# Recurrent attention with a wave-mixing layer on one core: weight loads without gating copies, weight tables in halves, and a new written order

## The chip, the cores and the metric

The kernel runs on one core of a Trainium2 chip. The core has a matmul engine (PE, with its weight loads PEld), a vector engine (DVE), an activation engine (ACT), GpSimd (POOL) and a sync engine that here only issues transfers (SP). SP and POOL each have a queue of transfers of their own; the transfers of both run on the core's 16 DMA engines. The metric is device time in microseconds; of several runs the median counts.

## The reference

The first part is a linear attention with decay, over 4 batches, 8 heads, 768 steps and heads of 48:

```python
for t in range(S):
    kt, vt, rt = (k[:, :, t], v[:, :, t], r[:, :, t])
    cur = np.einsum('bhd,bhe->bhde', u[None] * kt, vt)
    y[:, :, t] = np.einsum('bhd,bhde->bhe', rt, state + cur)
    state = w[None, :, :, None] * state + np.einsum('bhd,bhe->bhde', kt, vt)
```

Its result, x of 768 tokens by 384 columns in each batch, goes through a mixing layer:

```python
theta = x @ w_theta
zr, zi = x * np.cos(theta), x * np.sin(theta)
y = np.einsum('ts,bsd->btd', w_tok_r, zr) + np.einsum('ts,bsd->btd', w_tok_i, zi)
u = x + y
return u + np.maximum(u @ w_ch, 0.0)
```

## The kernel before

**The attention** goes over the tokens in chunks of 128, two chunks (a pair) at a time, three pairs in a batch (`front`). For each pair SP loads k and v in two transfers each and r in one. Kw is k times a table of inverse powers of w (`wpinv`), Rw is r times a table of powers (`wpow`), both in bf16 (L457, on POOL or DVE as the order says). PE transposes them (L416), ACT or DVE copies the transposes out as KT and RT (L206, L207). The scores KT by RT (L487) are masked by DVE into mAT (L492). PD is RT times KT (L497), from which PE makes the diagonal term dg (L504), and yd is dg times vb (L512), vb being v in bf16. The state grows by Kw by vb (L525), a DVE step (L539 or L541), a product with w^128 (L547) and two copies Sb in bf16 (L206, L207). The output y is RT by Sb (L560) and mAT by vb (L569) added up in one PSUM bank, and DVE adds yd to give x (L583). x is transposed, multiplied by Wth (theta, L605), ACT takes sine and cosine (L609), and DVE makes the two products z (L612).

**The mixing** (`mixing`) multiplies z by the transposed token weights WrT and WiT (L641) into uT (L652), then by Wch (L685); DVE adds the result to the transposed uT (L690) and SP stores it. Batch 0 mixes in single tiles of 128 tokens, so a tile needs only its own tile of WrT and WiT; the others mix 384 or 256 tokens at once.

**The weights.** POOL loads Wth and Wch (L384) and twelve tiles of token weights into six staging buffers (L395), casting them to bf16 on the way. PE transposes each tile (L402), ACT or DVE copies it out to WrT or WiT. None of these loads has an input to wait for. In the version before, a one-column copy from a loaded buffer into the destination (`after`, L375 to L379) makes the first load of each buffer wait: Wth for the first half of v of pair 0, six staging buffers and Wch for the first half of k of pair 2 of batch 0.

**The tables.** w is spread over the partitions by one matmul (L274), ACT takes the logarithm (L314) and three exponentials, `wpinv` and two of `wpow` (L319).

**The order.** Each piece of work is a task with a number, given in the order of the code. `ORDER`, a string that a search on a model of the chip wrote, lists the tasks in the order in which they are emitted, with the engine of each (P, V for DVE, A, G for POOL, S) and the PSUM banks of those that need one. Each engine runs its own tasks in that order, each when its inputs are there. A list entry such as `187G` is a whole task: here the load of a weight tile. POOL tasks that share a port with DVE (`port=True`) also wait for the last such DVE task that stands before them in the string (L135 to L138). The load buffers form a ring of ten, so a load of a later batch waits until the buffer has been read.

In the old string POOL's first fourteen entries are identity, iota, pads, mask, the first products Kw and Rw and a small one; then the copies and Wth, and the token loads behind a yd. SP's list begins with k, k, r of pair 0, then k, k, r of pair 1, r and a k of pair 2, and then v of pair 0.

Of the kernel before, what the change touches and what calls it, by code (L numbers as in the profile page):

```python
# [33 lines left out]
111P32 114P 112P 70P6 147P5 107V 144V 115V 113V 183G 170G 171G 108G 175G 148V 139A 76A 75A 71A 109A 150P4
151V 152G 154A 153A 72A 140P02 116P7 145V 117V 216S 188P3 192P5 142V 141V 110G 118P4 122P1 149G 189A 119A
193A 120A 77V 73V 124A 155P72 156P 158P 180P6 367P0 184P3 368P 185A 123A 159V 157V 181V 172P5 160P2 215S
214S 217S 261S 218S 262S 263S 265S 310S 264S 309S 206G 209G 200G 173A 360P4 361P 176P7 121V 203G 220G 161V
125V 222V 221V 219V 15G 162P6 166P3 353P1 177A 362P 354P 363P 355P 225P2 163A 164A 168A 167A 165V 169V 223P5
369P 370P 364P 226A 227A 224V 234V 231P76 232V 228P32 365P 356P 357P 238P5 366V 233V 239V 242V 266G 268G
235P7 371P 372P 241A 229V 267G 240G 270P4 373V 230V 376P6 358P 359V 236A 207P5 246P7 249P 247P3 210P0 378P2  # L40
374P1 271A 208V 403P4 201P5 377V 211A 202A 404P 405P 406P 407P 408P 204P6 311S 312S 313S 426S 473S 213G 197G
194G 375A 269V 237V 250V 248V 379A 205A 409V 316G 396P0 272P5 414P1 251P7 397P 398P 399P 400P 401P 243V 274G
273A 252A 244A 281V 285P2 275P34 278P65 314G 402V 282P7 286V 287G 245A 283A 288A 276V 290V 415A 280V 277V
253P0 412P7 254A 255A 257P3 318P2 315G 289G 317G 279V 294P15 258A 259A 383P4 384V 260V 386P0 295P 198P6
320P3 319A 321A 291G 284G 293A 292A 322A 413A 199V 195P4 380P2 297P 196V 387V 381V 296V 298V 389P6 390P 391P
392P 393P 394P 256V 299P4 395V 329V 333P3 326P02 323P15 419P7 385S 388S 382S 334V 324V 300A 301P6 330P4 303A
420V 327V 325V 328V 422P3 410P1 416P7 305P0 425S 335G 432G 337G 336A 302A 331A 430G 429S 428S 306A 304V 307A
438A 411V 423V 417V 332G 474S 472S 421S 424S 427S 418S 475S 521S 476S 619S 620S 522S 520S 621S 523S 524S
338P64 339P 434P5 341P 574P2 564P0 565P 569P1 449P3 599P7 342V 340V 343P4 435A 479G 570P 344A 480V 478V 477V
450V 453V 308V 483P5 481P6 349P4 482V 484A 345P3 604P5 600P 351A 350A 347A 346A 433V 431V 486P64 575P 436P3  # L50
352V 348V 451A 437A 492V 576P 577P 571P 601P 493P3 572P 487V 454G 456A 485A 494A 566P 445V 578V 488V 573V
527G 623S 489P62 442P34 496P1 452A 495G 490V 567P 446P6 605P 497V 491V 498G 568V 443V 602P 444V 501V 603V
583P2 457P0 447A 455A 448G 528G 526G 584A 499A 606P 607P 500A 608V 439P63 441V 440V 579P2 505P41 460P 581P7
508P 506P 591P5 525G 624G 502G 504G 625G 626G 582V 531P3 458P6 529P7 592V 580A 532A 533A 509V 507V 461V 459V
585P2 588P5 530A 622S 594P1 595P 462P3 510P4 586V 589V 631A 511A 503A 463V 540V 534P06 537P27 544P5 642P3
545V 546G 627G 548A 547A 596P 597P 541P4 468P5 542A 538V 536V 598V 643V 535V 539V 543G 646V 549P26 469A 470A
629P4 630A 464P1 550P 593S 667S 671G 645G 516P0 552P 512P5 610P7 551V 553V 466A 465A 513A 514A 587S 590S
628S 665S 609S 666S 673V 467V 471V 554P3 632P42 635P16 675P5 555A 634V 515V 644G 670G 672G 518A 517A 560P3
556P2 676A 561A 558A 562A 557A 636V 637V 611V 633V 647V 563V 638V 668S 669S 713S 712S 755P0 756P 765P1 650P5
616P6 780P7 781P 760P3 653P 613P4 639P2 766P 761P 559V 519V 614V 677A 640V 617V 641V 688P4 767P 689V 768P  # L60
654V 769V 651P2 790P6 719G 690V 717G 762P 763P 782P 783P 693V 652V 764V 784V 648A 649A 694G 696G 692A 691G
695A 612S 674S 684V 615S 618S 714S 681P51 678P42 682V 683V 680V 679V 791P 792P 685P3 793P 697P75 757P 758P
794V 759V 718G 720G 722P1 698P 686A 687G 785P3 700P 786P 787P 723A 699V 701V 715S 716S 724G 721S 731V 735P2
736V 728P46 725P01 774P7 732P5 656S 661P2 788P 655S 729V 730V 727V 726V 789V 733A 737G 738G 739G 740P45 743P
657P6 741P 771P1 734G 744V 702S 704P0 799P3 802P5 662A 663A 659A 658A 703S 708P2 706A 705A 770S 664V 742V
660V 746S 707V 777P6 810P4 796P0 709A 710A 775V 772V 778V 711V 805P7 806P 811P 751P2 815P1 752A 753A 745S
795S 773S 779S 776S 754V 747P6 816P 845P2 846P 748A 749A 750V 830P6 812P 813P 807P 808P 817P 818P 797V 803V
800V 814V 809V 819V 831P 835P0 847P 848P 840P5 841P 842P 836P 849V 854P3 862P4 843P 832P 833P 837P 838P 855V
863V 834V 844V 839V 824P7 821P1 827P2 850P3 852P4 856P6 798S 804S 801S 820S 825V 822V 828V 864S 826S 823S
829S 859P5 865P0 851A 853A 857V 860V 866V 858S 861S 867S  # L70
# [73 lines left out]
def kernel(  # L144
# [120 lines left out]
    def setup():  # L265
# [3 lines left out]
        def wu_fill(e):  # L269
# [4 lines left out]
        P.add((PE, 1300), lambda e: nc.tensor.matmul(bank("w")[:, :HD], ones, w_row, start=True,  # L274
                                                     stop=True),
              rd=["w_row", "ones"], acq=["w"], prio=-100, mode=3)
# [31 lines left out]
        def mask(e):  # L308
# [5 lines left out]
        P.add((ACT, 450), lambda e: nc.scalar.activation(  # L314
            lw_f, bank("w")[:, :HD], Act.Ln), rd=["tab0"], use=["w"],
              wr=["lw_f"], prio=-97.9)
        for j, (dst, col, key) in enumerate(((wpinv, 1, "wpinv"), (wpow[:, 0], 2, ("wpow", 0)),
                                             (wpow[:, 1], 3, ("wpow", 1)))):
            P.add((ACT, 520), lambda e, dst=dst, col=col: nc.scalar.activation(  # L319
                dst, lw_f, Act.Exp, scale=tok_f[:, col:col + 1]),  # L320
                rd=["lw_f", "tok_f"], wr=[key], prio=-97.7 + 0.1 * j)
# [51 lines left out]
    nstage, gate = [0], []  # L373

    def after(dst, load_key, key, prio):  # L375

        _, i, c = load_key
        P.add((POOL, 90), lambda e: nc.gpsimd.tensor_copy(dst, Ls[i][:, c * HD:c * HD + 1]),
              rd=[load_key], wr=[key], prio=prio, port=True)  # L379

    def weights(src, dst, key, prio, load_key):
        s3 = src.rearrange("(o p) n -> p o n", p=C)
        after(dst[:, 0, 0:1], load_key, key, prio)
        P.add((POOL, 850), lambda e: nc.gpsimd.dma_start(out=dst, in_=s3), wr=[key], prio=prio,  # L384
              dma=1700, kind="sw", port=True)

    def token_weights(prios, load_key):
        for to in range(NCH):
            for src, dst, key in ((moe_w_tok_r, WrT, "WrT"), (moe_w_tok_i, WiT, "WiT")):
# [3 lines left out]
                if nstage[0] <= 6:  # L393
                    after(stg[i][:, 0:1], load_key, ("stg", i), prio - 10)
# [34 lines left out]
    def front(b, base):  # L429
# [3 lines left out]
        for pr in range(NP):  # L433
# [10 lines left out]
            if b == 0 and pr == 0:  # L444
                load_wu()
                small_tables()
                weights(moe_w_theta, Wth, "Wth", -50, ("L", iv, 0))
            if b == 0 and pr == 2:
                gate.append(("L", ik, 0))
            for c in range(2):  # L450
                for src, tab, tk_, dst, key in (
                        (Ls[ik].rearrange("p (c h d) -> p c h d", c=2, h=H)[:, c], wpinv, "wpinv",
                         Kw, kK),
                        (Ls[ir].rearrange("p (h c d) -> p c h d", c=2, h=H)[:, c], wpow[:, c],
                         ("wpow", c), Rw, kR)):
                    P.add([(POOL, pool_ns(HD)), (DVE, dve_ns(HD))],
                          lambda e, c=c, src=src, tab=tab, dst=dst: eng_of[e].tensor_mul(  # L457
                              dst[:, c, :, :D], src, tab.rearrange("p (h d) -> p h d", h=H)),
                          rd=(L2(ir) if dst is Rw else [("L", ik, c)]) + [tk_], wr=[key + (c,)],
                          prio=pb, port=True)  # L460
# [241 lines left out]
    token_weights([20 + 4 * i for i in range(NCH)], gate[0])  # L702
    weights(moe_w_ch, Wch, "Wch", 50, gate[0])
# [37 lines left out]
```

## Time and profile before

| | |
|---|---|
| time, median of 3 runs | 136.4 us (136.21 to 136.49) |
| the profiled execution's own time | 137.21 us |
| its span | 135.5 us |
| PE busy | 122.2 us, 90% |
| DVE busy | 114.2 us, 84% |
| ACT busy | 78.0 us, 58% |
| POOL busy | 68.8 us, 51% |
| DMA moved | 24.65 MB, mean 182 GB/s |
| SP's queue (q1), POOL's queue (q0) | 21.44 MB and 2.95 MB |
| a k or v transfer, an r transfer | 192 KB, 384 KB |
| a token weight tile, Wth or Wch | 192 KB, 288 KB |

A busy share is the time in which an engine had an instruction in work. PE's time includes matmuls that wait in its pipeline. A row of the timeline gives the start, the duration, engine, line, operation, output, input and count of a group of instructions, and in brackets how long the engine was idle before it and what released it. In a row of busy time by stage stand the stage, its length, the busy time and instructions of PE, PEld, DVE, ACT and POOL, the granted clock, the mean share of the DMA engines (above 1 where transfers overlap) and GB/s. In a row of a DMA queue stand packets, MB, and the time of its packets as a share of the 16 engines' time in the window.

### The profile page before, as it was taken

The page shows a single profiled execution, that of the slowest core. Times are in us where ns is not written, and L with a number is a line of the kernel's source. Part 1 is how long each engine was busy: PE and PEld are TensorE (multiplying, and loading weights), DVE is VectorE, ACT ScalarE, POOL GpSimd, SP SyncE. Part 2 cuts the span into 40 slices and gives each one's busy share as a digit, 9 for nine tenths or more (in the row PEclk, how much of TensorE's full clock was granted, in tenths as well). Part 3 has the DMA queues.
Part 4 walks back from the last instruction along what each step waited for, and adds up shares of the span by engine and source line. Part 5 has one row for each costly group of instructions (what it writes and reads, how often), then busy time and mean ns, then how long its engine had stood idle before and what let it go on. Part 6 is the DMA issues. An engine that isn't in the chain of part 4 may idle for free.

```text
span 135.5 us, 4188 instructions
## 1 busy us (share of the span) xinstructions
PE 122.2 (90%) x1667; PEld 91.9 (68%) x1667; DVE 114.2 (84%) x231; ACT 78.0 (58%) x145; POOL 68.8 (51%) x104
## 2 busy tenths in 40 slices
PE   3358778979999999999999999999999999999990
PEld 1136665858989987977766687776566676577950
DVE  5279989798999869998999999999999997575581
ACT  3665868798836779858387339799411337240020
POOL 7324477767658456548205999755249860000000
PEclk9999999999999999999999999999999999999999
DMA  4999999999998993399999977997989439734945
GB/s 78 225 252 203 192 186 258 222 217 190 238 211 198 192 188 63 137 204 237 244 193 229 254 139 200 151 202 148 223 220 203 97 69 112 171 119 174 92 171 177
DMA packets 79781, 24.65 MB, mean 182 GB/s; under 512 B 74257, under 2 KB 79762, under 8 KB 79762
## 3 DMA queue, kind: packets, MB, share of 16 engines
q1 hardware_dynamic: 76400, 21.44, 75.4%
q0 software_dynamic: 2528, 2.95, 13.1%
q8 instruction: 13, 0.21, 0.6%
q10 hardware_dynamic: 834, 0.00, 0.3%
q14 instruction: 6, 0.05, 0.1%
HBM read 20.06 MB, written 4.72 MB: 183 GB/s over the span
## 4 chain that ended last, share of the span: by engine, by line
PE 68%; DVE 14%; DMA 8%; issue 3%; ACT 2%; SPq 1%; POOL 1%; DVEq 0%; POOLq 0%
PE bank L641 31%; PE bank L416 11%; PE bank L685 7%; PE bank L605 5%; DMA stg<-in_moe_w_tok_r_dram 5%; PE bank L487 4%; DVE mAT L492 4%; DMA ld<-in_r_dram 4%; PE bank L525 3%; PE bank L569 2%; PE bank L402 2%; PE bank L560 2%; ACT RT L206 2%; DVE z L612 1%; DVE fin L690 1%
## 5 line engine op out<-in xcount | busy, mean ns | idle before, releaser
L641 PEld LDWEIGHTS <-z 128*128 128x128 bf16 x468 | 34.3, 98 | 11.1 <-DVE z L612 0.4
L641 PE MATMUL bank<-WrT,z 128*128 128x128 bf16 (+2 forms) x234 | 31.8, 264 | 0.2 <-DVE z L612 0.2
L641 PE MATMUL bank<-WiT,z 128*128 128x128 bf16 (+2 forms) x234 | 31.8, 264 | 0.0
L492 DVE TENSOR_TENSOR mAT<-bank,mask 128x512 bf16<-128x512 f32 x48 | 31.0, 679 | 0.2 <-PE bank L487 0.2
L457 POOL TENSOR_TENSOR Kw<-ld,wpinv 128x384 bf16<-128x384 f32 x17 | 17.1, 1012 | 14.5 <-DVE yd L512 5.4
L612 DVE TENSOR_TENSOR z<-sc,x 128x768 bf16<-128x768 bf16 x24 | 14.2, 604 | 2.5 <-ACT sc L609 2.5
L605 PE MATMUL bank<-Wth,xT 128*128 128x384 bf16 x72 | 15.5, 334 | 0.9 <-DVE xT L207 0.6
L609 ACT ACTIVATE sc<-bank,pi 128x384 bf16<-128x384 f32 x24 | 13.9, 588 | 4.2 <-PE bank L605 3.5
L206 ACT ACTIVATE Sb<-St 64x192 bf16<-64x192 f32 x29 | 10.3, 358 | 9.8 <-DVE St L547 3.7
L206 ACT ACTIVATE RT<-bank 128x1024 bf16<-128x1024 bf16 x12 | 12.3, 1027 | 6.1 <-PE bank L416 6.0
L652 DVE TENSOR_TENSOR uT<-bank,xT 128x384 bf16<-128x384 f32 (+1 forms) x25 | 13.0, 534 | 2.9 <-PE bank L641 2.7
L685 PE MATMUL bank<-Wch,uT 128*128 128x384 bf16 (+2 forms) x75 | 14.7, 319 | 0.0
L512 POOL TENSOR_TENSOR yd<-dg,vb 128x768 bf16<-128x768 f32 x9 | 13.3, 1475 | 0.7 <-ACT sc L609 0.6
L547 POOL TENSOR_TENSOR St<-Ta,wC 128x192 f32<-128x192 f32 x12 | 6.7, 556 | 13.4 <-DVE Ta L541 6.2
L583 DVE TENSOR_TENSOR x<-bank,yd 128x384 bf16<-128x384 f32 x24 | 12.3, 549 | 1.4 <-POOL yd L512 0.8
L457 POOL TENSOR_TENSOR Rw<-ld,wpow 128x384 bf16<-128x384 f32 x12 | 11.9, 1002 | 2.5 <-DVE Rw L457 2.3
L609 ACT ACTIVATE sc<-bank 128x384 bf16<-128x384 f32 x24 | 11.4, 494 | 1.8 <-PE bank L605 1.8
L690 DVE SCALAR_TENSOR_TENSOR fin<-bank,un 128x384 f32<-128x384 f32 x21 | 10.8, 548 | 0.9 <-DMA un<-uT 0.7
L487 PE MATMUL bank<-RT,KT 64*128 64x128 bf16 x192 | 9.2, 235 | 2.0 <-ACT RT L206 2.0
L206 ACT ACTIVATE un<-bank 128x384 bf16<-128x384 bf16 x8 | 3.7, 484 | 11.7 <-PE bank L416 11.7
L497 DVE TENSOR_TENSOR PD<-RT,KT 128x1024 bf16<-128x1024 bf16 x12 | 8.2, 686 | 2.0 <-ACT RT L206 1.9
L206 ACT ACTIVATE KT<-bank 128x1024 bf16<-128x1024 bf16 x7 | 7.1, 1021 | 4.2 <-PE bank L416 4.2
(81 smaller groups left out, 199.6 us busy)
## 6 DMA issues: line engine op xcount, KB each, us to landing
ld<-in_k_dram SPq DMA_DIRECT2D x24, 192.0 KB, 4.6
ld<-in_r_dram SPq DMA_DIRECT2D x12, 384.0 KB, 4.8
ld<-in_v_dram SPq DMA_DIRECT2D x24, 192.0 KB, 4.7
out_dram<-fin SPq DMA_DIRECT2D x21, 192.0 KB, 2.0
stg<-in_moe_w_tok_r_dram POOLq DMA_DIRECT2D x6, 192.0 KB, 5.6
stg<-in_moe_w_tok_i_dram POOLq DMA_DIRECT2D x6, 192.0 KB, 5.5
out_dram<-stg SPq DMA_DIRECT2D x2, 192.0 KB, 1.9
Wth<-in_moe_w_theta_dram POOLq DMA_DIRECT2D x1, 288.0 KB, 5.7
```

The costliest lines, as they stand in the source:

```text
L206: return nc.scalar.activation(o, i, Act.Copy)
L416: nc.tensor.matmul(bank16(tok)[:, i * C:(i + 1) * C], s, ident, is_transpose=True, start=(i == 0), stop=(i == n - 1))
L457: lambda e, c=c, src=src, tab=tab, dst=dst: eng_of[e].tensor_mul(dst[:, c, :, :D], src, tab.rearrange("p (h d) -> p h d", h=H)),
L487: nc.tensor.matmul(bank(tk[hi])[:, hp * C:(hp + 1) * C], KT[q, c, hp, :], RT[q, hp, c, :], start=(hp == 0), stop=(hp == HP - 1))
L492: P.add((DVE, dve_ns(HP * C)), lambda e, hi=hi, tk=tk, mAT=mAT: nc.vector.tensor_mul(mAT[:, hi], bank(tk[hi]).rearrange("p (h t) -> p h t" ...
L512: lambda e, yd=yd, dg=dg, vb=vb: eng_of[e].tensor_mul(yd.rearrange("p a h d -> p (a h) d"), wide(dg, D), vb.rearrange("p a h d -> p (a h) ...
L605: nc.tensor.matmul(bank(th)[:, :HD], xT[:, dk, to * C:(to + 1) * C], Wth[:, dk, :], start=(dk == 0), stop=(dk == ND - 1))
L609: P.add((ACT, act_ns(HD) - 5 + 95 * (1 - ri)), lambda e, th=th, sc=sc, ri=ri: nc.scalar.activation(sc[:, ri], bank(th)[:, :HD], Act.Sin, * ...
L612: P.add((DVE, dve_ns(2 * HD, 2.0)), lambda e, sc=sc, to=to: nc.vector.tensor_mul(z[:, to], sc, bc(x[:, to], 1, 2)), rd=[("x", xi, to), ("s ...
L641: nc.tensor.matmul(bank(tm)[:, q * n * C:(q + 1) * n * C], z[:, so, ri, dk * C:(dk + 1) * C], WT[:, so, w], start=(s0 == 0 and ri == 0 and ...
L652: nc.vector.tensor_add(uT[:, dks[0]:dks[-1] + 1, w0:w1], bank(tm)[:, :len(dks) * (w1 - w0)].rearrange("p (d t) -> p d t", d=len(dks)), xT[ ...
L685: nc.tensor.matmul(bank(tf)[:, :(d1 - d0) * C], uT[:, dk, j * C:(j + 1) * C], Wch[:, dk, d0 * C:d1 * C], start=(dk == 0), stop=(dk == ND - 1))
```

## The change

Three things change. The `after` copies go, eight in all, with the arguments that named the load to wait for. The matmul that spreads w, the logarithm and `wpinv` are cut into two halves of columns, each half with a task of its own (`wpow` stays whole); Kw then waits for both halves of `wpinv`. And the order string is replaced.

```diff
-        P.add((PE, 1300), lambda e: nc.tensor.matmul(bank("w")[:, :HD], ones, w_row, start=True,
-                                                     stop=True),
-              rd=["w_row", "ones"], acq=["w"], prio=-100, mode=3)
+        halves = [slice(i * (HD // 2), (i + 1) * (HD // 2)) for i in range(2)]
+        for i, q in enumerate(halves):
+            P.add((PE, 650), lambda e, i=i, q=q: nc.tensor.matmul(
+                bank("w%d" % i)[:, q], ones, w_row[:, q], start=True, stop=True),
+                rd=["w_row", "ones"], acq=["w%d" % i], prio=-100, mode=3)
...
+        for i, q in enumerate(halves):
+            P.add((ACT, 290), lambda e, i=i, q=q: nc.scalar.activation(
+                lw_f[:, q], bank("w%d" % i)[:, q], Act.Ln), rd=["tab0"], use=["w%d" % i],
+                wr=[("lw_f", i)], prio=-97.9)
+        for dst, col, key, q, rd in [(wpinv[:, q], 1, ("wpinv", i), q, [("lw_f", i)])
+                                     for i, q in enumerate(halves)] + [
+                (wpow[:, j], 2 + j, ("wpow", j), slice(0, HD), [("lw_f", 0), ("lw_f", 1)]) for j in range(2)]:
...
-    def after(dst, load_key, key, prio):
-
-        _, i, c = load_key
-        P.add((POOL, 90), lambda e: nc.gpsimd.tensor_copy(dst, Ls[i][:, c * HD:c * HD + 1]),
-              rd=[load_key], wr=[key], prio=prio, port=True)
...
-        after(dst[:, 0, 0:1], load_key, key, prio)
...
-                if nstage[0] <= 6:
-                    after(stg[i][:, 0:1], load_key, ("stg", i), prio - 10)
```

The new string, read as tasks, differs in these places. POOL's list begins with three pads, iota, identity and a pad; then come the loads of WrT tile 2 and WiT tile 0, two pads, the loads of WrT tile 0, Wth and WiT tile 2, the mask, and only then the first Rw. WrT and WiT tile 1 follow behind vb of pair 0, tile 3 behind state products of pair 1, tiles 4 and 5 behind yd of pair 2. SP's list begins with k, k, r of pair 0, then r, k, k of pair 1, v, v of pair 0, v, v of pair 1, and then pair 2. PE's list has the transposes of Rw of both first pairs ahead of the first scores, and the first weight transpose among the scores of pair 1; its first mixing stands ahead of the KT transposes of pair 2. DVE's list has the first products z behind one Rw of pair 2, where the old list had much of pair 2 ahead of them. Between engines, three vb casts move from ACT to POOL, three Kw from POOL to DVE and three Rw from DVE to POOL, and a few copies and a state product trade places.

More of the change, by code (lines that the diff above doesn't have):

```diff
@@ L34 @@
[L34 to L48, printed above, removed]
@@ L313, in setup @@
         P.add((POOL, 600), mask, wr=["mask"], prio=-95)
[L314 to L321, printed above, removed]
+        for i, q in enumerate(halves):
[5 more added lines that the diff above has]
+                (wpow[:, j], 2 + j, ("wpow", j), slice(0, HD), [("lw_f", 0), ("lw_f", 1)]) for j in range(2)]:
+            P.add((ACT, act_ns(q.stop - q.start, False) + 105), lambda e, dst=dst, col=col, q=q: nc.scalar.activation(
+                dst, lw_f[:, q], Act.Exp, scale=tok_f[:, col:col + 1]),
+                rd=rd + ["tok_f"], wr=[key], prio=-97.7)
     def small_tables():
@@ L446, in front @@
                 small_tables()
-                weights(moe_w_theta, Wth, "Wth", -50, ("L", iv, 0))
-            if b == 0 and pr == 2:
-                gate.append(("L", ik, 0))
+                weights(moe_w_theta, Wth, "Wth", -50)
             for c in range(2):
                 for src, tab, tk_, dst, key in (
-                        (Ls[ik].rearrange("p (c h d) -> p c h d", c=2, h=H)[:, c], wpinv, "wpinv",
+                        (Ls[ik].rearrange("p (c h d) -> p c h d", c=2, h=H)[:, c], wpinv, ("wpinv", 0),
                          Kw, kK),
@@ L458, in front @@
                               dst[:, c, :, :D], src, tab.rearrange("p (h d) -> p h d", h=H)),
-                          rd=(L2(ir) if dst is Rw else [("L", ik, c)]) + [tk_], wr=[key + (c,)],
+                          rd=(L2(ir) if dst is Rw else [("L", ik, c), ("wpinv", 1)]) + [tk_], wr=[key + (c,)],
                           prio=pb, port=True)
@@ L701 @@
     front(0, 0)
-    token_weights([20 + 4 * i for i in range(NCH)], gate[0])
-    weights(moe_w_ch, Wch, "Wch", 50, gate[0])
+    token_weights([20 + 4 * i for i in range(NCH)])
+    weights(moe_w_ch, Wch, "Wch", 50)
     for b in range(B):
```

75 lines of the change are left out of this document (45 added, 30 removed).

## The prediction

> **What bounds the kernel now.** I read the page's head and chain first, then busy time by stage, then the chain piece by piece.
>
> ```profile
> span 135.5 us, 4188 instructions
> PE 68%; DVE 14%; DMA 8%; issue 3%; ACT 2%; SPq 1%; POOL 1%; DVEq 0%; POOLq 0%
> ```
>
> ```profile
> core 0: us, PE busy (x) PEld busy (x) DVE busy (x) ACT busy (x) POOL busy (x), PEclk, DMA share, GB/s
> 0.00:10.00 10.00, 4.04 (x26) 2.30 (x26) 5.00 (x16) 5.45 (x7) 4.98 (x18) 1.00 0.84 182
> 10.00:20.00 10.00, 7.83 (x114) 6.55 (x109) 9.28 (x20) 6.92 (x11) 5.05 (x12) 1.00 1.02 195
> 20.00:33.00 13.00, 11.61 (x184) 9.01 (x182) 11.53 (x24) 11.19 (x22) 9.09 (x15) 1.00 1.18 223
> 33.00:82.00 49.00, 48.96 (x791) 39.59 (x789) 45.19 (x90) 32.27 (x61) 30.19 (x35) 1.00 0.90 192
> 82.00:98.00 16.00, 16.00 (x209) 10.95 (x207) 15.95 (x32) 13.43 (x26) 9.07 (x12) 1.00 1.03 192
> 98.00:132.00 34.00, 33.74 (x359) 23.51 (x358) 26.66 (x56) 8.76 (x19) 10.45 (x13) 1.00 0.74 142
> ```
>
> From 33 us on PE has no gap. From 82 to 98 DVE has none either (15.95 of 16.00), and there the chain runs over DVE. So the kernel is a ramp of 33 us and then a wall of PE work, with DVE just keeping up. The change alters neither the mixing nor any other matmul behind the ramp; it can gain in the ramp only, and can lose anywhere.
>
> ```profile
> 1.93 4.85 DMA ld<-in_r_dram
> ...
> 9.68 0.61 PE bank L487 x8
> 10.29 0.97 PE bank L416 x8
> ...
> 25.19 6.39 DMA stg<-in_moe_w_tok_r_dram
> ...
> 36.12 0.89 PE bank L416 x16
> ...
> 38.02 0.55 PE bank L487 x16
> ...
> 77.31 0.97 PE bank L641 x6
> ```
>
> Eight transposes take 0.97 us at 10 us and sixteen take 0.89 at 36 us, so early PE runs at half pace, though the granted clock is printed as 1.00 all along. At 77 us six 128x384 matmuls take 0.97, 162 ns each, end to end. The chain's two transfers, the first r and a weight tile, are what the change touches.
>
> ```profile
> 28.82 1.35 DVE L612 TENSOR_TENSOR z<-sc,x 128x768 bf16<-128x768 bf16 x2
> ```
>
> ```profile
> 30.23 0.51 PE L641 MATMUL bank<-WrT,z 128*128 128x128 bf16 x6 [0.24 <-DVE z L612]
> ```
>
> **The milestone** is the first mixing matmul, at 30.23 us, released by batch 0's first two z.
>
> **The removed copies.**
>
> ```profile
> 15.22 0.19 POOL L378 CAST stg<-ld 128x1 bf16<-128x1 f32 x1 [2.61 <-DVE Kw L457]
> 15.85 0.95 POOL L384 DMA_DIRECT2D Wth<-in_moe_w_theta_dram  x1 [0.32 <-POOL Wth L378]
> 20.02 0.59 POOL L395 DMA_DIRECT2D stg<-in_moe_w_tok_r_dram  x1 [0.79 <-DVE x L583]
> ```
>
> ```profile
> 1.40 0.56 POOL L300 MEMSET Kw<- 128x256 bf16 x2
> ```
>
> Eight casts of 0.19 us, 1.5 us in all, beside a POOL that is busy half of the span: worth nothing by themselves. What they did was to keep Wth until 15.85 and the first token tile until 20.02. In the new order POOL has only three pads, iota, identity and a pad ahead of the first weight load. At 0.28 us a pad (the row), from 0.8 us on, that is about 2.6 us. Five loads follow by about 6.4 us: WrT tile 2, WiT tile 0, WrT tile 0, Wth, WiT tile 2. Nothing in front of them waits. (A cast of the first r, Rw, stands behind them on POOL until 6.9 us; with SP at half of the bytes, as below, that r lands at 3.2 + 0.57/0.118 + 1.1 = 9.1, so the issues themselves cost nothing.) "Held back by their place" therefore holds back very little, and the five share the DMA engines with the first k and r.
>
> ```profile
> q1 hardware_dynamic: 1155, 0.22, 36.4%
> ```
>
> ```profile
> q1 hardware_dynamic: 5721, 1.60, 100.1%
> ```
>
> ```profile
> q0 software_dynamic: 229, 0.33, 92.7%
> q1 hardware_dynamic: 573, 0.12, 27.6%
> ```
>
> ```profile
> q0 software_dynamic: 891, 1.15, 65.8%
> q1 hardware_dynamic: 5154, 1.17, 54.5%
> ```
>
> These are SP's queue (q1) in 0 to 3.2 us and in 3.2 to 10, then POOL's (q0) and SP's in 22 to 24 and in 20 to 30. From 3.2 us SP alone fills the engines: 1.60 MB in 6.8 us, 0.235 MB/us. With weight loads in flight SP keeps 0.12 of 0.45 MB (27%) or 1.17 of 2.32 (50%).
>
> **The delay of the first loads.**
>
> ```profile
> ld<-in_r_dram SPq DMA_DIRECT2D x12, 384.0 KB, 4.8
> stg<-in_moe_w_tok_r_dram POOLq DMA_DIRECT2D x6, 192.0 KB, 5.6
> ```
>
> SP's new list begins k, k (192 KB each), r of pair 0, r of pair 1: 1.18 MB. The five weight loads are 1.08 MB. PE's new order wants RT of pair 1 ahead of the scores of pair 0, so the second r is what counts. Of 2.26 MB, 0.22 are moved by 3.2 us; 2.04 at 0.235 take 8.7 us more, to 11.9. Before, the first r's last byte is due by the same working at 5.6 us and it landed at 6.78: a lag of 1.1. So the second r lands at **13.0** where all five weight loads go first; with SP at 50% of the bytes the transfer ends at 3.2 + 0.96/0.118 = 11.3, landing 12.4. Without any contention it would be 3.2 + 0.96/0.235 + 1.1 = 8.4, the other end. I take 12.8, because the measured shares lie at 27 and 50%.
>
> [...]
>
> **From the second r to the first z.**
>
> ```profile
> 6.88 1.03 DVE L457 TENSOR_TENSOR Rw<-ld,wpow 128x384 bf16<-128x384 f32 x2 [0.37 <-DMA ld<-in_r_dram]
> ```
>
> ```profile
> L492 DVE TENSOR_TENSOR mAT<-bank,mask 128x512 bf16<-128x512 f32 x48 | 31.0, 679 | 0.2 <-PE bank L487 0.2
> L612 DVE TENSOR_TENSOR z<-sc,x 128x768 bf16<-128x768 bf16 x24 | 14.2, 604 | 2.5 <-ACT sc L609 2.5
> L457 DVE TENSOR_TENSOR Rw<-ld,wpow 128x384 bf16<-128x384 f32 x12 | 7.3, 637 | 0.5 <-DMA ld<-in_r_dram 0.4
> L583 DVE TENSOR_TENSOR x<-bank,yd 128x384 bf16<-128x384 f32 x24 | 12.3, 549 | 1.4 <-POOL yd L512 0.8
> L497 DVE TENSOR_TENSOR PD<-RT,KT 128x1024 bf16<-128x1024 bf16 x12 | 8.2, 686 | 2.0 <-ACT RT L206 1.9
> L512 DVE TENSOR_TENSOR yd<-dg,vb 128x768 bf16<-128x768 f32 x3 | 3.1, 1048 | 0.0
> L541 DVE TENSOR_TENSOR Ta<-bank,St 128x192 f32<-128x192 f32 x16 | 5.6, 352 | 1.0 <-POOL St L547 0.5 <-PE bank L525 0.3
> ```
>
> 12.8 + two Rw on DVE 1.03 + transposes 0.97 + two score groups at 0.61, with some 0.1 of hand-over, gives 16.0. From there DVE's new list to the second z is 8 mAT, 4 state updates, PD, 4 x, yd, two evacuations of 0.55, Rw, dg, 2 z: by the rows 5.4 + 1.4 + 0.7 + 2.2 + 1.05 + 1.1 + 0.6 + 0.2 + 1.2 = 13.9, less 0.07 to 0.08 by which neighbours overlap (Rw: two in 1.03) for 24 of them, 12.1. First z pair at **28.1**, if this list never waits; POOL's and ACT's work for it (vb, Sb, sin) fits beside.
>
> **What PE has done by then.** Ahead of the first mixing PE's old list holds, beyond the new one's, one k flip (0.45 at full pace, from the 16 in 0.89), two score groups (0.55), a diag and an outer of about 0.2 each, an inter of 0.35 and two intras of 0.4, and it lacks one weight flip (0.35): 1.8 us. The new order breaks even on PE if its first mixing starts at 30.2 - 1.8 = 28.4. At 28.1: **-0.3 us**.
>
> **What DVE has done by then.** The old list ahead of that z has 4 mAT, one Kw, Rw, PD, two state steps and a dg more and one evacuation less: by start-to-start time 2.4 + 1.1 + 0.6 + 0.55 + 0.1 - 0.5 = 4.3 us. Over the whole kernel the new order gives DVE 0.4 us less (three Kw and a KT evacuation more, three Rw, two weight evacuations, a St and a dg less). DVE breaks even at 30.2 - 4.3 + 0.4 = 26.3; at 28.1 it is 1.8 behind. Between 33 and 82 us it idles 3.8 us, which may swallow this; from 82 to 98 it has no slack at all. Ends 0 and 1.8; I take half, **+0.9**, since the idle time lies in pieces beside waits for PE.
>
> **Tables in halves.**
>
> ```profile
> 3.88 0.49 ACT L314 ACTIVATE lw_f<-bank 128x384 f32<-128x384 f32 x1 [0.34 <-PE bank L274]
> ```
>
> ```profile
> 5.10 1.00 POOL L457 TENSOR_TENSOR Kw<-ld,wpinv 128x384 bf16<-128x384 f32 x1 [1.61 <-ACT wpinv L319]
> ```
>
> Kw waits for this table now. Half a row costs more than half of 0.49, so four half steps end near 5.1 again: from 0.5 earlier to 0.5 later, and hidden behind r, which is later. Zero. Three vb casts that move from ACT to POOL, and the tail, which keeps its shape (three chan groups behind the last mixing, as before): zero, both have idle time beside them.
>
> **Sum.** -0.3 + 0.9 = +0.6; with 0.2 for DVE waits that the list does not show, +0.8 us. The profiled execution's 137.21 (span 135.5 and 1.7 around it) becomes 138.0; it stands 0.8 above the median of the runs, 136.4, so the forecast is **137.2**.
>
> **Rivals.** *The weight loads fit in* (not slower, 25%). SP's ring is ahead of POOL's by 1.8 us, and its requests hold the engines. For: from 3.2 us SP alone needs the engines for two more loads only. Against: the 27%. If SP keeps 60%, the second r lands at 3.2 + 0.96/0.141 + 1.1 = 11.1, the first z pair at 26.4: PE -2.0, DVE 0.1 behind; 134.4 to 134.6. The point from which it decides is 12.1: there the z pair comes at 27.4, PE -1.0, and DVE's half of 1.1 with the 0.2 nearly cancels it.
>
> *DVE's list waits* (slower, 17%). The new order puts a weight flip and an intra between two score groups, and the casts of Kw on POOL behind DVE's. Were 1.3 us of waits in the list, z comes at 29.4: PE +1.0, DVE +1.6: 139.0. For: DVE's 82 to 98 row. Against: 9.28 of 10 busy in 10 to 20 us before.
>
> *PE reaches full pace earlier* (faster, 7%). [...]
>
> *Both effects cancel* (within 0.2%, about what a measurement of this kernel can tell from no change): 9%. That the change does not do what it says: the loads could start late only if POOL waited, and nothing ahead of them does.
>
> **Numbers.** Forecast 42%: its own range 136.7 to 138.3. Faster 25 + 7 = 32%, same 9%, slower 42 + 17 = 59%. The range reaches into the first rival and past the second: 134.5 to 139.3. The far end of the delay, no contention at all, would put z at 23.7 and the time near 132; the 27 and 50% rows leave it under 5%, and it stays out.
>
> **What would show it.** Right: first weight issue on POOL by 3 us; SP's queue at half or less of the bytes from 3.5 to 10 us; the first r later than 8 us, the second near 13; the first z pair near 28; PE gapless afterwards, DVE busier than 45 of 49 in the middle. Wrong: the second r before 12, z by 27, or gaps in PE after 35 us.

## The result and the profile after

The changed kernel takes 147.49 us (median of 4 runs, 145.97 to 148.98) against 136.44 (136.21 to 136.7): a ratio of 1.0772, 95% interval 1.0676 to 1.0868. (Ratios here and below leave out single runs in a slower state, here the one of 148.98 us, so they can be smaller than the quotient of the medians.) That is slower, as forecast, but by 10.5 to 11 us where 0.8 was forecast, and far above the range. The profiled execution took 148.02 us, with a span of 146.3.

First the ramp. These are rows of the timeline of the kernel after, on POOL, DVE and PE; to compare, the kernel before has the first Rw at 6.88 (the two products of the first r in one row), the first z at 28.82 and the first mixing at 30.23. The load rows are the first and the last of the five; the row at 14.04 is the second r.

```profile
2.48 0.72 POOL L390 DMA_DIRECT2D stg<-in_moe_w_tok_r_dram  x1
...
5.50 0.59 POOL L390 DMA_DIRECT2D stg<-in_moe_w_tok_i_dram  x1
```

```profile
7.63 0.56 DVE L450 TENSOR_TENSOR Rw<-ld,wpow 128x384 bf16<-128x384 f32 x1 [1.26 <-DMA ld<-in_r_dram]
14.04 1.03 DVE L450 TENSOR_TENSOR Rw<-ld,wpow 128x384 bf16<-128x384 f32 x2 [5.85 <-DMA ld<-in_r_dram]
...
28.28 1.25 DVE L450 TENSOR_TENSOR Rw<-ld,wpow 128x384 bf16<-128x384 f32 x1
29.46 1.02 DVE L605 TENSOR_TENSOR z<-sc,x 128x768 bf16<-128x768 bf16 x2
```

```profile
30.53 0.84 PE L634 MATMUL bank<-WrT,z 128*128 128x128 bf16 x12 [0.32 <-DVE z L605]
```

The weight loads are issued from 2.48 us, the first r is there at 7.6, the second at 14.0 after 5.85 us in which DVE stands still, and the first mixing starts at 30.53, 0.3 us later than before. On its own that would cost 2 or 3 us, as the experiments show. The rest is lost where the forecast had PE without a gap. Busy time by stage (stage, length, PE, PEld, DVE, ACT, POOL, granted clock, DMA share, GB/s):

```profile
10.00:20.00 10.00, 4.51 (x65) 3.40 (x66) 5.21 (x10) 4.90 (x8) 5.34 (x8) 1.00 1.13 217
20.00:33.00 13.00, 11.37 (x167) 8.83 (x165) 12.27 (x23) 9.57 (x18) 7.73 (x11) 1.00 1.08 211
33.00:82.00 49.00, 44.99 (x731) 36.57 (x730) 45.00 (x77) 31.40 (x57) 27.14 (x34) 0.97 0.76 160
82.00:98.00 16.00, 14.94 (x198) 9.95 (x195) 15.80 (x29) 8.39 (x18) 11.51 (x14) 1.00 0.77 175
```

From 33 to 82 us PE had 48.96 us of work in 791 instructions; now it has 44.99 in 731. DVE's busy time looks as before, 45.00 against 45.19, but it holds 77 instructions where there were 90. DVE isn't busier with more work, its instructions are longer. The groups by line say which ones (count, busy us, mean ns):

```profile
L490 DVE TENSOR_TENSOR PD<-RT,KT 128x1024 bf16<-128x1024 bf16 x12 | 9.2, 763 | 0.2
L450 DVE TENSOR_TENSOR Rw<-ld,wpow 128x384 bf16<-128x384 f32 x9 | 8.9, 998 | 7.1 <-DMA ld<-in_r_dram 7.1
L450 DVE TENSOR_TENSOR Kw<-ld,wpinv 128x384 bf16<-128x384 f32 x10 | 8.4, 852 | 1.7 <-DMA ld<-in_k_dram 1.7
L505 DVE TENSOR_TENSOR yd<-dg,vb 128x768 bf16<-128x768 f32 x3 | 3.6, 1215 | 0.0
L534 DVE TENSOR_TENSOR Ta<-bank,St 128x192 f32<-128x192 f32 x16 | 5.6, 353 | 0.6 <-PE bank L518 0.2 <-PE bank L480 0.2
```

Rw went from a mean of 637 ns to 998, Kw from 670 to 852, PD from 686 to 763, yd from 1048 to 1215: products whose two inputs both lie in SBUF. (z is one too and didn't rise, 604 before and 593 after; both means lie above the 553 that it takes in `fill_late` below.) Ta, with one input in PSUM, stays at 352 to 353. The worst single row, with what POOL ran at that time and what PE waited for:

```profile
39.77 3.09 DVE L450 TENSOR_TENSOR Rw<-ld,wpow 128x384 bf16<-128x384 f32 x1
42.78 1.34 DVE L450 TENSOR_TENSOR Kw<-ld,wpinv 128x384 bf16<-128x384 f32 x1
```

```profile
39.67 0.86 POOL L207 CAST vb<-ld 128x768 bf16<-128x768 f32 x1
40.45 1.98 POOL L450 TENSOR_TENSOR Rw<-ld,wpow 128x384 bf16<-128x384 f32 x2
42.37 1.34 POOL L450 TENSOR_TENSOR Kw<-ld,wpinv 128x384 bf16<-128x384 f32 x1
```

```profile
44.65 1.03 PE L411 MATMUL bank<-ident,Rw 128*128 128x128 bf16 x8 [2.92 <-DVE Rw L450]
```

A product of 0.55 us takes 3.09 because POOL starts a cast 0.1 us earlier and two products behind it. DVE gets through when they are done (40.45 + 1.98 = 42.43). PE then stands idle for 2.92 us, and its next eight transposes take 1.03 us; the same eight took 0.62 at 29.59. If from every DVE instruction the shortest one of the same kind and shape is taken off, what is left is its stretch. All together DVE lost 5.1 us to it in the kernel before and **11.6 us** after. (The expectations below were written with a count over merged rows, which gave 4.1 or 4.2 and 11.1.)

### The profile page after: what moved, and what is told of

It is laid out like the page before. It is cut to its first block, busy times and chain, and to the rows that moved or that the text cites. A ratio compares the mean times of both kernels' runs of the same rounds, so it can differ in the third digit from the quotient of the medians.

```text
span 146.3 us, 4177 instructions
## 1 busy us (share of the span) xinstructions
PE 124.3 (85%) x1669; PEld 92.0 (63%) x1669; DVE 120.1 (82%) x229; ACT 77.7 (53%) x144; POOL 72.1 (49%) x101
## 5 line engine op out<-in xcount | busy, mean ns | idle before, releaser
L634 PEld LDWEIGHTS <-z 128*128 128x128 bf16 x468 | 34.9, 99 | 10.8 <-DVE z L605 0.5
L540 POOL TENSOR_TENSOR St<-Ta,wC 128x192 f32<-128x192 f32 x13 | 6.6, 509 | 28.1 <-DVE Ta L534 24.9
L206 ACT ACTIVATE RT<-bank 128x1024 bf16<-128x1024 bf16 x12 | 12.3, 1026 | 11.1 <-PE bank L411 11.0
L450 POOL TENSOR_TENSOR Rw<-ld,wpow 128x384 bf16<-128x384 f32 x15 | 15.9, 1067 | 4.8 <-DMA ld<-in_r_dram 3.0
L450 POOL TENSOR_TENSOR Kw<-ld,wpinv 128x384 bf16<-128x384 f32 x14 | 15.1, 1085 | 5.0 <-PE bank L598 1.8
L411 PE MATMUL bank<-ident,Rw 128*128 128x128 bf16 x96 | 8.8, 241 | 9.6 <-DVE Rw L450 9.3
L598 PE MATMUL bank<-Wth,xT 128*128 128x384 bf16 x72 | 14.9, 327 | 0.7 <-DVE xT L207 0.4
L450 DVE TENSOR_TENSOR Rw<-ld,wpow 128x384 bf16<-128x384 f32 x9 | 8.9, 998 | 7.1 <-DMA ld<-in_r_dram 7.1
L411 PEld LDWEIGHTS <-Rw 128*128 128x128 bf16 x96 | 6.6, 107 | 11.7 <-DVE Rw L450 10.6
L602 ACT ACTIVATE sc<-bank 128x384 bf16<-128x384 f32 x24 | 11.4, 488 | 3.6 <-PE bank L598 3.2
L576 DVE TENSOR_TENSOR x<-bank,yd 128x384 bf16<-128x384 f32 x24 | 12.6, 549 | 0.6 <-POOL yd L505 0.5
L683 DVE SCALAR_TENSOR_TENSOR fin<-bank,un 128x384 f32<-128x384 f32 x21 | 11.1, 551 | 0.5 <-DMA out_dram<-fin 0.3
L206 ACT ACTIVATE KT<-bank 128x1024 bf16<-128x1024 bf16 x6 | 6.1, 1024 | 7.9 <-DVE x L576 4.8
```

The lines of the kernel that those rows point to most:

```text
L206: return nc.scalar.activation(o, i, Act.Copy)
L411: nc.tensor.matmul(bank16(tok)[:, i * C:(i + 1) * C], s, ident, is_transpose=True, start=(i == 0), stop=(i == n - 1))
L576: P.add((DVE, dve_ns(HD)), lambda e, c=c, to=to, ty=ty, yd=yd: nc.vector.tensor_add(x[:, to], bank(ty[c])[:, :HD], yd[:, c].rearrange("p h ...
L598: nc.tensor.matmul(bank(th)[:, :HD], xT[:, dk, to * C:(to + 1) * C], Wth[:, dk, :], start=(dk == 0), stop=(dk == ND - 1))
L602: P.add((ACT, act_ns(HD) - 5 + 95 * (1 - ri)), lambda e, th=th, sc=sc, ri=ri: nc.scalar.activation(sc[:, ri], bank(th)[:, :HD], Act.Sin, * ...
L634: nc.tensor.matmul(bank(tm)[:, q * n * C:(q + 1) * n * C], z[:, so, ri, dk * C:(dk + 1) * C], WT[:, so, w], start=(s0 == 0 and ri == 0 and ...
```

## The experiments

Two theories stood against each other. **A**: the early weight loads delay the first r, DVE falls behind, and a full DVE never makes it up. **B**: DVE's products with two inputs in SBUF stand still while POOL runs its own products or casts, and the new order lets them meet. A third, **C**, came up on the way: a store at the head of SP's queue makes later loads late.

### The first loads behind POOL's first Rw: `late_w`

```diff
-11G 8G 12G 5G 7G 13G 184G 175G 14G 9G 172G 37G 187G 17G 41G 36G
+11G 8G 12G 5G 7G 13G 14G 9G 17G 41G 184G 175G 172G 37G 187G 36G
```

This is POOL's part of the new order; 184, 175, 172, 37 and 187 are the five weight loads and 41 is the first Rw.

> The new kernel with its five first weight loads put behind POOL's first Rw (issued from about 9 us, not 2.5). Theory A (the early loads delay the second r to 14.0 us, DVE falls 4 us behind, and DVE sets the end from then on): the second r lands at 8 to 9.5 us, the first z pair ends at 25 to 27 instead of 30.5, and the time falls by 3 to 5 us, to 142.5 to 144.5. Theory B (what costs is that DVE and POOL run two-input products at the same time and hold each other up, 39 to 46 us and later): the time falls by less than 1.5 us.

Measured: 144.7 us (143.3 to 145.31), ratio 1.0582 (1.0518 to 1.0646).

```profile
7.20 1.36 DVE L444 TENSOR_TENSOR Rw<-ld,wpow 128x384 bf16<-128x384 f32 x2 [0.51 <-DMA ld<-in_r_dram]
...
26.57 1.01 DVE L599 TENSOR_TENSOR z<-sc,x 128x768 bf16<-128x768 bf16 x2
...
36.86 3.07 DVE L444 TENSOR_TENSOR Rw<-ld,wpow 128x384 bf16<-128x384 f32 x1
39.86 1.34 DVE L444 TENSOR_TENSOR Kw<-ld,wpinv 128x384 bf16<-128x384 f32 x1
```

The second pair of Rw comes at 7.2 us instead of 14.0 and the first z at 26.57, 2.9 us earlier than after and 2.2 earlier than before. The time falls by 2.8 us. But the kernel is still 8 us slower than before although its ramp is now shorter, and the rows of 3.07 and 1.34 us are there again, 2.9 us earlier. The fall lies between the two expectations, and the early loads explain a quarter of the loss.

### POOL's four tasks moved behind DVE's: `apart`

```diff
-222G ... 262G 264G 263G ... 217V 214V 215V ... 261G 208G 216V
+... 217V 214V 215V ... 261G 208G 216V 222G 262G 264G 263G
```

> The new kernel with POOL's vb of batch 1 pair 0 and three products of pair 1 put behind DVE's four products of pair 0 in the order, so that the two engines do not run them at the same time at 40 to 45 us. Theory B: DVE's Rw of 3.09 us and Kw of 1.34 us take 0.55 each, PE's wait of 2.9 us at 41.7 goes, and the time falls by 2.5 to 4 us, to 143.5 to 145. Theory A: at most 1 us less, since DVE is behind anyway.

Measured: 148.65 us (147.37 to 148.95), ratio 1.0864 (1.0806 to 1.0923): no gain. The timeline of this run on DVE, then on POOL:

```profile
39.60 0.55 DVE L444 TENSOR_TENSOR Rw<-ld,wpow 128x384 bf16<-128x384 f32 x1
40.06 0.55 DVE L444 TENSOR_TENSOR Kw<-ld,wpinv 128x384 bf16<-128x384 f32 x1
...
41.49 5.80 DVE L599 TENSOR_TENSOR z<-sc,x 128x768 bf16<-128x768 bf16 x2
```

```profile
43.18 0.84 POOL L201 CAST vb<-ld 128x768 bf16<-128x768 f32 x1
43.97 1.95 POOL L444 TENSOR_TENSOR Rw<-ld,wpow 128x384 bf16<-128x384 f32 x2
45.88 0.99 POOL L444 TENSOR_TENSOR Kw<-ld,wpinv 128x384 bf16<-128x384 f32 x1
```

Rw and Kw are back at 0.55 us, but the two z behind them, 1.01 us elsewhere, take 5.80. The first of them, 1.33 us, meets the POOL Kw ahead of these four tasks (41.17 to 42.41); the second, 42.75 to 47.29, stands until all four are done. The meeting was moved, not removed. The time speaks against the gain that B expected here, the rows speak for its mechanism, so it had to be tested by removal.

### The copies alone, and the early loads alone, in the old order: `old_nocopy`, `old_early`

`old_nocopy` turns the eight copies of the kernel before into nothing; `old_early` does that too, and moves its first five weight loads ahead (in the second diff the emptied copies are left out).

```diff
-        P.add((POOL, 90), lambda e: nc.gpsimd.tensor_copy(dst, Ls[i][:, c * HD:c * HD + 1]),
-              rd=[load_key], wr=[key], prio=prio, port=True)
+        P.add((POOL, 90), lambda e: None, rd=[], wr=[key], prio=prio)
```

```diff
-6G 4G 8G 10G 16G 7G 11G 13G 12G 36G 9G ...
+6G 4G 8G 10G 16G 7G 11G 13G 187G 191G 179G 183G 35G 12G 36G 9G ...
```

> The old kernel without its eight copies, the order untouched: the first part of the change alone. Both theories: Wth is issued at about 12.7 instead of 15.9 us, the token tiles stay behind the yd at 17 us, nothing lands on the first r; 136.0 to 137.0. A rival that the copies themselves kept the ramp in order: 138 or more.

> The old kernel without its copies, with its first five weight loads moved to the head of POOL's queue, ahead of its products, as the new order has them. Theory A: its r and k of the first pairs land 3 to 5 us later, the first z pair goes from 30.2 to 32 to 34, and the time rises by 2 to 5 us, to 138.5 to 141.5. Theory B: less than 1 us, since the products of DVE and POOL stand apart in the old order.

Measured: `old_nocopy` 135.89 us (135.5 to 136.46), ratio 0.9958 (0.9938 to 0.9978); `old_early` 141.63 (141.07 to 141.88), ratio 1.0366 (1.0339 to 1.0394). In the latter DVE waits 6 us for a k that it waited 0.46 us for in the kernel before; the row of before, then that of `old_early`:

```profile
8.37 0.94 DVE L457 TENSOR_TENSOR Kw<-ld,wpinv 128x384 bf16<-128x384 f32 x1 [0.46 <-DMA ld<-in_k_dram]
```

```profile
14.19 0.56 DVE L451 TENSOR_TENSOR Kw<-ld,wpinv 128x384 bf16<-128x384 f32 x1 [6.03 <-DMA ld<-in_k_dram]
```

So dropping the copies is worth 0.6 us as long as the order keeps the loads late (in `old_nocopy` the first is issued at 15.21 us), and early loads cost 1.0366 - 0.9958 = 0.0408, or 5.6 us, in an order that isn't made for them. There A's expectation is borne out and B's, less than 1 us, is not. The new order, which has the r of pair 1 early in SP's list, loses only half as much to them, 2.2 to 2.8 us.

### DVE does the work itself: `own_b1`

```diff
 (on top of late_w)
-222G 262G 264G 263G ... 216V
+222G ... 216V 262V 264V 263V
```

> The new kernel with the five first weight loads behind POOL's first Rw (as in late_w, 144.7 us) and three products of batch 1 (Rw, Rw, Kw of pair 1) given from POOL to DVE, behind DVE's own four of pair 0. Theory A (DVE is late and full, what POOL does beside it costs nothing): DVE gets three products of 0.47 us more, so 144.7 to 146.1. Theory B (a product of two SBUF inputs on DVE stands still while POOL runs one): the 3.07 and 1.34 us rows of late_w fall to about 1.4 and 0.55, 2.3 to 3.4 us less against 1.4 more; PE's wait of 2.90 us for Rw shrinks: 142.2 to 143.7.

Measured: 142.78 us (141.54 to 143.81), ratio 1.0430 (1.0376 to 1.0484): 2 us less than `late_w`, though the fullest engine got three products more.

```profile
37.30 1.18 DVE L444 TENSOR_TENSOR Rw<-ld,wpow 128x384 bf16<-128x384 f32 x1
...
39.81 1.82 DVE L444 TENSOR_TENSOR Rw<-ld,wpow 128x384 bf16<-128x384 f32 x2
```

The row of 3.07 us is 1.18 (beside the cast that stayed on POOL), and two of the products taken over last 1.82 (beside a Kw that stayed there). Theory A expected a loss. It falls as an account of the part after 33 us.

### SP's loads ahead of the store: `sp`

```diff
 (on top of late_w)
-... 376V 383S 469S ... 467S 468S ... 471S ... 470S 515S 518S 517S 516S ... 519S
+... 376V 469S 467S 468S 471S 470S 515S 518S 517S 516S 519S 383S ...
```

> late_w with ten loads of batch 2 (r, k, v of its pairs 1 and 2) ahead of the first store in SP's list; before, that store waited for its DVE result and the ten loads behind it. Theory C (the store at the head of SP's queue makes the r of batch 2 pair 2 late, so POOL's products are late and meet DVE's at 79 to 83 us): DMA no longer idle at 60 us, POOL's wait of 2.0 us for r gone, DVE's stretch of 2.5 us at 79 to 83 gone: 142 to 143.5. Theory A or B without C: 144.7 within 0.5.

Measured: 146.33 us (146.31 to 146.71), ratio 1.0727 (1.0704 to 1.0750), slower than `late_w` and in none of the ranges expected. The loads do go out early (from about 52 us), POOL no longer waits for r, and the three DVE rows that stood 2.4 us beside POOL at 79 to 83 us in `late_w` are back at their plain length; but POOL's three products then run straight into DVE's z, one of which takes 3.08 us:

```profile
77.77 4.01 DVE L599 TENSOR_TENSOR z<-sc,x 128x768 bf16<-128x768 bf16 x3 [0.72 <-ACT sc L596]
```

```profile
77.52 0.99 POOL L444 TENSOR_TENSOR Rw<-ld,wpow 128x384 bf16<-128x384 f32 x1
78.47 1.00 POOL L444 TENSOR_TENSOR Kw<-ld,wpinv 128x384 bf16<-128x384 f32 x1
79.43 1.00 POOL L444 TENSOR_TENSOR Rw<-ld,wpow 128x384 bf16<-128x384 f32 x1
```

The meeting was moved again: 2.5 us of stretch in one z for 2.4 in three rows. In all DVE's stretch is 11.4 us here and 12.6 in `late_w`, so it doesn't explain why the time rose. Of the 1.2 us between the two profiled spans (144.6 and 143.4) 0.8 is there already at the Rw of 37.65 (36.86 in `late_w`), ahead of the first load that was moved; its cause stays open. Theory C finds no support: the late r was real, and bringing it forward gained nothing.

### The old order without its edges: `noport`

```diff
-                tc.add_manual_dep(ins.ins, last.ins.name, SYNC, reason="shared port")
+                pass
```

> The kernel before without the edges that make a POOL task wait for the last such DVE task ahead of it in the order; nothing else changed. Theory B: POOL's products and casts start earlier and meet DVE's; DVE's stretch, 4.2 us in the kernel before, doubles, and the time is 138 to 142. Theory A: the edges only delay POOL, which is half idle; 136.4 within 0.5, or a little faster.

Measured: 141.15 us (138.57 to 142.37; the executions lie far apart and no interval was formed, but the lowest is 2.1 us above the kernel before). In its trace a yd of 0.95 us takes 2.53 beside a cast and a Kw on POOL:

```profile
44.17 2.53 DVE L507 TENSOR_TENSOR yd<-dg,vb 128x768 bf16<-128x768 f32 x1
```

```profile
43.75 1.18 POOL L202 CAST vb<-ld 128x768 bf16<-128x768 f32 x1
44.90 0.99 POOL L452 TENSOR_TENSOR Kw<-ld,wpinv 128x384 bf16<-128x384 f32 x1
```

The old order and the edges together keep the two engines off each other, all but the 5.1 us of stretch in the kernel before. The edges hold in one direction only: POOL waits for the DVE task ahead of it in the string, and no DVE task waits for POOL. They don't help where POOL's tasks stand ahead of DVE's in the string, as those of 39.67 us do in the new kernel (222, 262, 264 and 263 in the diff of `apart`): nothing there makes DVE's product wait for them.

### The cost by itself: `micro`

A kernel of seven stages, each with four DVE instructions, computes nothing of the reference.

> Nothing of the reference is computed; the output is zeros. Seven stages on DVE, each one sum from PSUM and then four instructions: f32 products with two SBUF inputs alone; the same beside three POOL products; sums with one PSUM input beside three POOL products; z products (bf16) beside three POOL products; f32 products beside two POOL casts; beside four POOL weight loads; PSUM copies beside three POOL products. Theory B: stages 2, 4 and 5 are longer by the time that POOL is busy (one instruction of 2.5 to 3.5 us in stages 2 and 4), stages 3, 6 and 7 are not. Theory A: all as long as without POOL, 0.5 to 0.6 us per instruction.

The groups by line:

```profile
L103 DVE TENSOR_TENSOR dv<-fa,fb 128x384 bf16<-128x384 f32 x4 | 4.1, 1071 | 0.0
L113 DVE TENSOR_TENSOR dv<-ha,hb 128x768 bf16<-128x768 bf16 x4 | 4.0, 1053 | 0.0
...
L118 DVE TENSOR_TENSOR dv<-fa,fb 128x384 bf16<-128x384 f32 x4 | 2.8, 768 | 0.0
L98 DVE TENSOR_TENSOR dv<-fa,fb 128x384 bf16<-128x384 f32 x4 | 2.0, 553 | 0.0
L123 DVE TENSOR_TENSOR dv<-fa,fb 128x384 bf16<-128x384 f32 x4 | 2.0, 554 | 0.0
L108 DVE TENSOR_TENSOR dv<-bank,ha 128x384 bf16<-128x384 f32 x4 | 2.0, 550 | 0.0
L128 DVE CAST dv<-bank 128x384 bf16<-128x384 f32 x4 | 2.0, 550 | 0.0
```

Alone (L98) a product takes 553 ns. Beside three POOL products it takes 1071 (L103), a z 1053 (L113); beside two casts 768 (L118). Sums and copies from PSUM (L108, L128) and products beside POOL's weight loads (L123) are untouched, at 550 to 554. B's direction holds in every stage; its form (one instruction of 2.5 to 3.5 us) doesn't: here the engines took turns, the longest DVE product being 1.34 us, and POOL's second and third product took 1.30 instead of 0.99.

### POOL's products replaced by memsets: `fill_new`, `fill_late`, `fill_old`

In the kernel after, in `late_w` and in the kernel before, each POOL product Rw, Kw or yd and each cast vb becomes a one-column copy and memsets of like length, so these kernels leave out part of the computation:

```diff
+    def fill(dst, read, n):
+        ins = nc.gpsimd.tensor_copy(one[:, :read.shape[-1]], read)
+        if n:
+            nc.gpsimd.memset(scr[:, :n], 0.0)
+        nc.gpsimd.memset(dst, 0.0)
+        return ins
...
-                          lambda e, c=c, src=src, tab=tab, dst=dst: eng_of[e].tensor_mul(
+                          lambda e, c=c, src=src, tab=tab, dst=dst: fill(
+                              dst[:, c, :, :D], src[:, 0, 0:1], 520) if e == POOL else eng_of[e].tensor_mul(
```

> The new kernel; POOL's products Rw, Kw, yd and its casts vb are left out, each replaced by a one-column copy of its input and memsets of its output and of a scratch tile that last as long, in the same places of the same order with the same waits. DVE's work is untouched. Theory B (what DVE loses beside POOL's products is the larger part of the loss): DVE's stretch falls from 11.1 to under 3 us, the rows of 3.09 and 1.34 us to 0.55, and the time from 147.5 to 139.5 to 142; what is left above the kernel before is the 2.8 us of the early loads and little else. Theory A (late start and a full DVE): 147.5 within 1.

> The same replacement in late_w (five first weight loads behind POOL's first Rw). Theory B: from 144.7 to 136.5 to 139, the kernel before's time or little above. Theory A: 144.7 within 1.

> The same replacement in the kernel before, whose DVE rows are stretched by 4.1 us in all. Theory B: that stretch goes too, but PE is gapless there from 33 us, so 135 to 136.4. Theory A: 136.4 within 0.3.

Measured: `fill_new` 139.7 us, ratio 1.0201 (1.0130 to 1.0271); `fill_late` 137.25, ratio 1.0038 (1.0013 to 1.0063); `fill_old` 136.06, ratio 0.9953 (0.9935 to 0.9971). All three lie where B put them, and the first two far from A's ranges. `fill_late` by stage and at the place of the 3.07 us row:

```profile
33.00:82.00 49.00, 48.78 (x798) 39.09 (x796) 45.17 (x90) 34.91 (x63) 32.87 (x84) 1.00 0.93 198
82.00:98.00 16.00, 16.00 (x208) 11.06 (x207) 15.58 (x35) 13.48 (x27) 9.19 (x27) 1.00 0.88 183
```

```profile
37.04 0.56 DVE L455 TENSOR_TENSOR Rw<-ld,wpow 128x384 bf16<-128x384 f32 x1
```

PE is gapless again, DVE's 45.17 us hold 90 instructions, and its stretch over the whole run is 1.0 us. With these the loss can be shared out (ratios times 136.5 us; the intervals leave some 1.6 us on the first share and 1 us on the second). Taking POOL's products out saves the new order 0.0772 - 0.0201 = 0.0571, or 7.8 us, and the old one 0.0047, or 0.6 us: **7.2 us of the loss are meetings of POOL and DVE** and what follows from them. Moving the loads back saves a further 0.0201 - 0.0038 = 0.0163, **2.2 us**. What is left between `fill_late` and `fill_old`, 0.0085 or 1.2 us, is the new order's other differences; no run looked into those. By the way they are formed the three add up to the whole, 0.0772 or 10.5 us.

### The tables in halves: `old_halves`

```diff
 (on top of old_nocopy)
+        def ln_exp(e):
+            for q in halves:
+                nc.scalar.activation(lw_f[:, q], bank("w")[:, q], Act.Ln)
+                nc.scalar.activation(wpinv[:, q], lw_f[:, q], Act.Exp, scale=tok_f[:, 1:2])
```

> The kernel before without its eight one-column copies (as in old_nocopy, 135.9 us) and with the tables in halves: two matmuls of half a row, then logarithm and power of each half, in that order. Both theories: the second half of the table is ready at 5.07 us in the kernel after and the whole one at 5.0 in the kernel before, so 135.9 within 0.3. If the halves are worth something by themselves, the first Kw starts before 4.9 us and the time falls below 135.6.

Measured: 136.41 us (135.63 to 136.96), ratio 0.9973 (0.9953 to 0.9992), which can't be told from `old_nocopy`. The halves gain nothing that can be told: here the power of the second half runs from 4.94 to 5.40 us, where the whole row's ran from 4.40 to 5.01.

The version that beats both kernels is therefore `old_nocopy`, the kernel before by 0.4%: the old order, with its weight loads held back by their place alone, without the copies.

## Why the prediction was wrong, point by point

**What held.** The weight loads start before 3 us (2.48), nothing holds them back, and the five share the DMA engines with the first k and r. The removed copies and the halves are worth next to nothing: 0.6 us and nothing. (Half a row's logarithm took 0.33 us in the kernel after where the whole row's had taken 0.49, its power 0.45 and 0.46 where it had been 0.61. The eight copies took 1.8 us of POOL, not 1.5: six of 245 ns on average and two of 0.19 us.) That the kernel got slower was forecast, but the sum that gave this sign had the ramp at -0.3 and most of the loss in no term, so the sign is more luck than working.

**The second r, close and by another way.** It was taken at 12.8 and came at 14.0, behind the late end of its bounds (13.0). SP's queue did not move half or less from 3.5 to 10 us: it had 0.80 of 1.43 MB, 56%. Only from 10 to 13 us did it fall to 0.14 of 0.58 MB, 24%. The prediction took one share for the whole time; the queue's share changed in between. The first r wasn't held up as forecast: 7.6 instead of later than 8.

**The ramp, mis-sized.** The first z pair was put at 28.1, if the list never waits. It ended at 30.48: 1.2 us from the later r, 0.7 from the Rw of 28.28 that met a POOL product, the rest from waits. By the prediction's own break-even (28.4) the first mixing at 30.53 means 2.1 us lost on PE; the runs give the early loads 2.2 to 2.8. The term stood at -0.3.

**The step that failed** is the one on DVE: "it is 1.8 behind ... Ends 0 and 1.8; I take half, +0.9", and ahead of it "POOL's and ACT's work for it (vb, Sb, sin) fits beside". DVE's list was summed with the mean durations of before, as if they belonged to the instructions. They belong to the instructions in that order: the same Rw is 0.56 us, 1.25 or 3.09 according to what POOL does meanwhile. So an edit that moves POOL against DVE has a cost of its own, and 1.8 us was no upper bound for it: the one row of 3.09 us alone stood 2.5 us. The term measured 7.2 us. The "zero" for three vb casts that move to POOL fails with it: the cast at 39.67 us begins the worst meeting.

The trace of before showed the effect, in a row that wasn't read beside its neighbour:

```profile
33.45 1.55 DVE L457 TENSOR_TENSOR Rw<-ld,wpow 128x384 bf16<-128x384 f32 x1
```

```profile
33.56 1.01 POOL L457 TENSOR_TENSOR Rw<-ld,wpow 128x384 bf16<-128x384 f32 x1
34.50 1.71 POOL L305 MEMSET Sb<- 128x1920 bf16 x1
```

1.55 us beside a POOL product, three times the 0.52 of the row at 6.88; and the next two Kw on DVE, beside the memset, took 1.01 together. The code hinted at it too: by their name, "shared port", the edges were put in against such a meeting. What the two engines share, a port or something else, no run shows; the runs show how long each stood.

**PE gapless after 33 us** fails for the same reason: 4.0 us idle from 33 to 82 and 1.1 from 82 to 98. The wall of PE work was a property of the old order.

**The rivals.** "DVE's list waits" had the right sign and engine, at the wrong place (the ramp) and at 139.0. None of the rivals had a product on POOL that holds up one on DVE; the one on DVE's list names POOL's Kw only as something that DVE might wait for. As to *PE reaches full pace earlier*: in the kernel after six transposes of x still took 0.81 us at 24.17 and 0.50 at 27.20; in the one before three theta matmuls took 1.14 at 22.42 and 0.65 at 24.69. What sets this pace, no run shows. Of the 10.5 us, 1.2 belong to no step that could be named: they are left when meetings and early loads are taken out.

## What to carry to other kernels

Before a new order of work is priced, look at each long instance of a group, not its mean, and see which other engine was running at that moment. If two engines slow each other, their relative timing is a cost term, and one meeting can cost about the other's unbroken run (the longest stand here was 4.0 us, beside 3.7 us of POOL work). When busy time stays the same and the count falls, as from 90 instructions in 45.19 us to 77 in 45.00 here, look for what holds the engine up; giving the off-loaded work back to the full engine can be faster (in `own_b1` three products of 0.47 us more went with 4.0 us less of stretch, 8.6 for the 12.6 of `late_w`). To test such a cause, remove it; moving it only shows the next victim.

## What the runs showed of the hardware

- DVE's products with two SBUF inputs and POOL's products and casts hold each other up. In `micro` DVE's product took 553 ns alone, 1071 beside POOL's products and 768 beside its casts, and POOL's second and third product 1.30 us where the first took 0.99. DVE's sums with one input in PSUM and its copies from PSUM, beside as many POOL products, stayed at 550 ns, its products beside POOL's weight loads at 554, and in `fill_late` an Rw beside a memset (37.06, 0.78 us) at 0.56 us. In this pair of the kernel after, DVE's product began first, and it was POOL's that stretched, to 1.24 us:

```profile
44.52 0.54 DVE L450 TENSOR_TENSOR Kw<-ld,wpinv 128x384 bf16<-128x384 f32 x1
```

```profile
44.67 1.24 POOL L450 TENSOR_TENSOR Kw<-ld,wpinv 128x384 bf16<-128x384 f32 x1 [0.97 <-DVE Rw L450]
```

  But five DVE products that began 0.11 to 0.43 us ahead of POOL's, while POOL was still issuing a load, stood all the same, 1.0 to 4.0 us: the Rw at 33.45 of the kernel before, the z at 42.75 of `apart`, and one each in `old_nocopy`, `old_early` and `old_halves`. A z of `noport` (31.50) took its plain 0.55 us in such a place; why isn't known.
- A DVE product can stand through more than one POOL instruction. It waited for a cast and two products (3.09 us), for three products (`sp`, one z of 3.08), and in `apart` a z took 4.54 us beside a cast and three products; in `micro` the two took turns, the longest DVE product being 1.34 us. What decides between these wasn't found.
- The idle PE of the kernel after paid twice. Behind the 2.92 us gap eight transposes took 1.03 us, where the eight at 29.59 took 0.62, and the granted clock (the number ahead of the DMA share) was down to a half:

```profile
45.00:47.00 2.00, 2.00 (x22) 2.00 (x20) 1.80 (x3) 1.02 (x1) 1.68 (x2) 0.50 1.02 201
```

  In `late_w`, behind a gap of 2.90 us, eight transposes took 0.64 us, but the six matmuls after them 0.82 (six took 0.50 in `fill_late`), and the granted clock of 33 to 82 us was 0.97, as in the kernel after. Behind a gap of 1.88 us (`own_b1`, before 43.10) six matmuls took 0.51 and the clock stayed at 1.00 from 43 to 49 us. What decides between these, no run shows.
